# A fused attention, FFN and top-1 expert kernel: the first half of the FFN in five blocks of 256 tokens and two of 512 instead of nine of 256

## The chip, the cores and the metric

The kernel runs on one core of a Trainium2 chip. The metric is the device time of one execution in microseconds (us). Engines are named as in the profile: PE (matrix multiplies; PEld is its weight load), DVE, ACT and POOL (elementwise work), SP (issues most transfers). Each engine works through its own instructions in the order in which the program holds them; waits between engines go by semaphores.

## What is computed

```python
def reference(q, k, v, f, w_in, w_out, expert_emb, tau, w1, w2):
    # attention with a forget gate: 4 batches, 8 heads, 576 tokens, head size 64
    scores = q @ k.T / 8 + (cum_i - cum_j)      # cum = cumsum(log f), causal
    x = softmax(scores) @ v                     # -> 2304 tokens x 512
    # FFN, 512 -> 2048 -> 512
    h = x @ w_in
    g = where(h >= 1, h, where(h <= -1, 0, (h + 1)**2 / 4))
    x = g @ w_out
    # top-1 mixture of 8 experts, 512 -> 1024 -> 512
    e = argmax(cosine(x, expert_emb) / tau); p = softmax(...)[e]
    return p * (relu(x @ w1[e]) @ w2[e])
```

All matrices are float32. The program reads `w_in` and `w_out` as float64 and splits each operand of the FFN and expert products into a high and a low part of the type fp32r, so that every product is three matmuls: high by high, high by low, low by high.

## The kernel before

**Stages.** The FFN is cut into two halves of 1024 hidden units each, because the weights of one half fill their buffers: `half0` (names with p: `hp`, `ghp`, `accp`) and `half1` (names with r). Each half passes over all 2304 tokens; `half0` writes its part of the result to DRAM as `x2p`, `half1` adds its own to it. Then `moe` runs the most frequent expert on all tokens (names with m), and small slots correct the others.

**Blocks.** `half0` has nine blocks of `TB` = 256 tokens (`px0` to `px8`), and `half1` and `moe` have five blocks of up to 512 (`WIDE`, `NW` = 5). A hidden chunk is 128 of the 1024 hidden units, so a block has eight (`NF` = 8). `run1` makes the hidden values: for each chunk 12 matmuls (`first`, L882) into a PSUM bank of 512 columns, which holds two chunks of a 256-token block or one chunk of a 512-token block; one filled bank is a *unit*. `run2` multiplies a chunk by the second weights: 12 matmuls into the accumulator (`ffn_second`, L1011). For 256 tokens the accumulator is one tile `acc`; for 512 tokens it is `acc` and `accB`, and `accB` lies in a pool that exists only after the attention.

**One unit's way** is called the hidden chain in this text: ACT reads the bank into `t` (`tp`, L894), DVE makes `g` in two steps (`gp`, L898 and L899), ACT rounds it to its high part (`ghp`, L903), POOL subtracts for the low part (`glp`, L904). There are two banks (`h_b`), one `t` (`t1_b`), one `g` (`t2_b`) and two pairs of `ghp` and `glp` (`g_b`), so a `ghp` waits until the matmuls of the unit two before it are done.

**Loads and results.** The input of a block is loaded from `xs` in DRAM, rounded by ACT and subtracted by DVE: `load_block` with one transfer and one step each for 256 tokens, `load_wide` with four of each for 512. Buffer 0 exists from the start; buffers 1 and 2 lie in the pool `gp`, which opens when the attention is done (`att_ok`, `late_pools`); a wide load takes buffer 2 or buffers 0 and 1 together. A block's result is taken out of PSUM by `ffn_finish0` (`x_0_n`, L1043 and L1044) and stored by `keep`.

**The second half's weights** are converted while `half0` works on its last blocks. There are 16 pieces (`float64_piece`, names `wbr`, `wbx`, `wb`), and each needs, one behind the other: ACT L825, DVE L826, L828, L830 and L832, ACT L836, POOL L837. All pieces share one buffer `wbx` (`wx_b` = 1), so ACT L825 of a piece waits for POOL L837 of the piece before. In this text piece 5 is the fifth.

**What sets the order.** The order of the instructions on every engine is fixed when the program is built: the class `Order` simulates the engines with estimated durations (`mm`, `act`, `dve`, `pool2`, `dma`) and emits an instruction when its simulated engine takes it. Work carries a priority: attention 0 to 1, hidden chains 2, conversion 4, `first` 6, `ffn_second` 6.5. On the chip the emitted order is kept, whatever the durations then are.

## Time and profile before

| | us |
|---|---|
| median of 3 runs | 866.98 (866.78 to 869.88) |
| the profiled execution's own time | 867.16 |
| its span, first to last instruction | 865.6 |
| PE busy | 844.3 |
| DVE, ACT, POOL busy | 464.6, 362.7, 304.2 |
| last matmul of the attention's weighted sum ends | 312.4 |
| first matmul of `half1` starts | 429.6 |

Busy time is a sum over instructions; a busy PE is one that has a matmul in flight. The chain of waits is followed back from the last instruction and names at each step what released it. PE's clock was granted in full over nearly the whole span (0.997).

### The profile page before, as it was taken

The page shows a single profiled execution, that of the slowest core. Times are in us where ns is not written, and L with a number is a line of the kernel's source. Part 1 is how long each engine was busy: PE and PEld are TensorE (multiplying, and loading weights), DVE is VectorE, ACT ScalarE, POOL GpSimd, SP SyncE. Part 2 cuts the span into 40 slices and gives each one's busy share as a digit, 9 for nine tenths or more (in the row PEclk, how much of TensorE's full clock was granted, in tenths as well). Part 3 has the DMA queues.
Part 4 walks back from the last instruction along what each step waited for, and adds up shares of the span by engine and source line. Part 5 has one row for each costly group of instructions (what it writes and reads, how often), then busy time and mean ns, then how long its engine had stood idle before and what let it go on. Part 6 is the DMA issues. An engine that isn't in the chain of part 4 may idle for free.

```text
span 865.6 us, 15076 instructions
## 1 busy us (share of the span) xinstructions
PE 844.3 (98%) x5384; PEld 693.4 (80%) x5384; DVE 464.6 (54%) x1108; ACT 362.7 (42%) x841; POOL 304.2 (35%) x407
## 2 busy tenths in 40 slices
PE   9999998999999999999899999999999999999997
PEld 7665776887777799999888888888898888887685
DVE  7797977666545537777754344467652531212121
ACT  5677766565556644434533243323343121212110
POOL 3566876555544442444432122222210033000000
PEclk9999999999999999999999999999999999999999
DMA  7997666574324235233611133645432111541220
GB/s 145 174 188 180 164 164 154 123 141 119 95 67 122 73 123 110 79 120 98 207 62 49 61 130 112 211 142 183 148 124 85 49 49 49 211 154 50 98 74 25
DMA packets 154251, 101.96 MB, mean 118 GB/s; under 512 B 102802, under 2 KB 125842, under 8 KB 154176
## 3 DMA queue, kind: packets, MB, share of 16 engines
q1 hardware_dynamic: 151008, 96.22, 40.8%
q0 software_dynamic: 2832, 4.22, 1.8%
q8 instruction: 43, 0.70, 0.4%
q10 hardware_dynamic: 336, 0.56, 0.2%
q14 instruction: 32, 0.26, 0.1%
HBM read 76.86 MB, written 24.49 MB: 117 GB/s over the span
## 4 chain that ended last, share of the span: by engine, by line
PE 82%; DVE 9%; POOL 3%; ACT 2%; issue 2%; DMA 2%; SPq 0%; ACTq 0%; DVEq 0%; POOLq 0%
PE hm L882 12%; PE hr L882 12%; PE hp L882 8%; PE accp L1011 7%; PE accr L1011 6%; PE accBr L1011 6%; PE accm L1023 6%; PE accBm L1023 6%; PE SR L534 4%; PE T L614 4%; PE X L654 4%; PE gt L1197 1%; DVE wbx L830 1%; POOL wb L837 1%; PE U L707 1%
## 5 line engine op out<-in xcount | busy, mean ns | idle before, releaser
L904 POOL TENSOR_TENSOR glr<-gr,ghr 128x512 fp32r<-128x512 f32 x36 | 47.3, 1315 | 147.3 <-PE accBr L1011 90.8
L600 POOL TENSOR_SCALAR P<-P,st 128x512 f32<-128x512 f32 (+3 forms) x128 | 77.0, 615 | 38.4 <-DVE st L596 25.1
L882 PE MATMUL hr<-rx,wb 128*128 128x512 f32 (+1 forms) x384 | 89.5, 367 | 0.0
L882 PE MATMUL hm<-mx,wm 128*128 128x512 f32 (+1 forms) x336 | 87.0, 379 | 0.0
L1011 PE MATMUL accp<-ghp,wa 128*128 128x256 f32 x576 | 83.4, 287 | 2.1 <-DVE x_7b L1044 1.7
L589 ACT ACTIVATE P<-P,st 128x512 f32<-128x512 f32 (+3 forms) x128 | 71.4, 559 | 32.8 <-DVE st L584 31.8
L913 DVE SCALAR_TENSOR_TENSOR glm<-hm,ghm 128x512 fp32r<-128x512 f32 x36 | 24.8, 689 | 103.1 <-PE accBm L1023 68.4
L1011 PEld LDWEIGHTS accp<-ghp,wa 128*128 128x128 f32 x576 | 73.7, 190 | 5.4 <-issue 2.2
L912 ACT ACTIVATE ghm<-hm 128x512 fp32r<-128x512 f32 x36 | 21.6, 599 | 132.5 <-PE accBm L1023 120.7
L882 PEld LDWEIGHTS hr<-rx,wb 128*128 128x128 f32 x384 | 65.6, 188 | 13.0
L882 PEld LDWEIGHTS hm<-mx,wm 128*128 128x128 f32 x336 | 61.0, 188 | 14.9 <-issue 3.4
L904 POOL TENSOR_TENSOR glp<-gp,ghp 128x512 fp32r<-128x512 f32 x36 | 48.8, 1357 | 60.7 <-ACT ghp L903 54.2
L584 DVE CUSTOM_DVE_ANT_0 P<-SR,cm 128x512 f32<-128x512 f32 (+3 forms) x96 | 45.1, 485 | 24.8 <-PE SR L534 22.2
L614 PE MATMUL T<-ident,P 128*128 128x128 f32 x320 | 52.4, 278 | 3.5 <-POOL P L600 2.9
L894 ACT ACTIVATE tr<-hr,quarter 128x512 f32<-128x512 f32 x36 | 24.7, 687 | 61.3 <-DVE gr L899 44.4
L634 ACT COPY pt<-T 128x512 f32<-128x512 f32 (+2 forms) x96 | 35.3, 391 | 36.0 <-PE T L614 35.3
L898 DVE SCALAR_TENSOR_TENSOR gr<-tr 128x512 f32<-128x512 f32 x36 | 25.9, 719 | 42.1 <-POOL glr L904 40.5
L614 PEld LDWEIGHTS T<-ident,P 128*128 128x128 f32 x320 | 36.8, 141 | 14.5 <-POOL P L600 6.3
L534 PE MATMUL SR<-kt,qt 64*128 64x384 f32 (+3 forms) x224 | 44.9, 478 | 2.8 <-DVE st L584 2.5
L1011 PE MATMUL accr<-ghr,wb 128*128 128x512 f32 (+1 forms) x160 | 47.0, 375 | 0.0
L1011 PE MATMUL accp<-glp,wa 128*128 128x256 f32 x288 | 46.3, 283 | 0.4 <-POOL glp L904 0.4
L1011 PE MATMUL accBr<-ghr,wb 128*128 128x512 f32 (+1 forms) x160 | 46.5, 372 | 0.0
(355 smaller groups left out, 1871.8 us busy)
## 6 DMA issues: line engine op xcount, KB each, us to landing
cm<-rows SPq DMA_DIRECT2D x24, 256.0 KB, 4.4
rawq<-in_q_dram SPq DMA_DIRECT2D x64, 72.0 KB, 3.9
rawk<-in_k_dram SPq DMA_DIRECT2D x64, 72.0 KB, 3.3
xs<-xT SPq DMA_DIRECT2D x16, 288.0 KB, 2.1
x2n<-nat SPq DMA_DIRECT2D x18, 256.0 KB, 4.9
war<-in_moe_w_in_dram SPq DMA_DIRECT2D x8, 512.0 KB, 4.7
war<-in_moe_w_out_dram SPq DMA_DIRECT2D x8, 512.0 KB, 4.6
rawv<-in_v_dram SPq DMA_DIRECT2D x32, 128.0 KB, 2.7
```

Source lines behind the costliest of these rows:

```text
L534: nc.tensor.matmul(bank[:, j, :w], qt[p, P * c:P * c + P], kt[p, :w], start=True, stop=i >= NSUM)
L584: yield dve(w + 80, lambda: nc.vector.tensor_tensor_reduce(out=pv_, in0=so, in1=m, scale=-0.125, scalar=3e38, op0=ALU.add, op1=ALU.min, ac ...
L589: yield act(w, lambda: nc.scalar.activation(pw, pw, AF.Exp, bias=st[:, n:n + 1], scale=-1.0, accum_out=st[:, 2 + n:3 + n]), 1, 330)
L600: yield pool1(w, lambda: nc.gpsimd.tensor_scalar(pw, pw, st[:, 6 + n:7 + n], 1.0, ALU.mult, ALU.mult), 0)
L614: nc.tensor.transpose(T[:, P * n:P * n + P], p[:, P * kb:P * kb + P], ident)
L634: yield act(n, lambda: nc.scalar.copy(dh, src), 0)
L654: nc.tensor.matmul(X[D * j:D * j + D, P * kb:], vt[:, kb, j], pt[i, j][0][:, 512 * kb:512 * kb + 512 - P * kb], start=(kb == 0), stop=(kb ...
L882: nc.tensor.matmul(oo, a[:, c, cs], x[c], start=(ip == 0 and c == 0), stop=(ip == 2 and c == KC - 1))
L898: yield dve(n, lambda: nc.vector.scalar_tensor_tensor(g, t, 0.5, t, ALU.min, ALU.mult), 2)
L904: yield pool2(n, lambda: nc.gpsimd.tensor_tensor(gl, g, f32(gh), ALU.subtract), 1)
L1011: nc.tensor.matmul(acc[d][:, :w], b[:, fc, P * d:P * d + P], g, start=(fc == 0 and ip == 0 and (not narrow or d % 2 == 0)), stop=(fc == NF ...
L1023: nc.tensor.matmul(acc[a * (4 // na)], g[:, P * a:P * a + P], b[:, fc], start=(fc == 0 and ip == 0), stop=(fc == NF - 1 and ip == 2))
```

## The change

`half0` keeps 256 tokens for its first five blocks and takes the last 1024 tokens as two blocks of 512. These two are loaded by `load_wide`, wait for the whole attention (`att_ok`), use `acc` and `accB`, and store their result with four transfers of 512 columns (`keep_first`).

```diff
+    NARROW = 5
+    FIRST = [(TB * n, TB) for n in range(NARROW)] + [
+        (t, 2 * TB) for t in range(TB * NARROW, NT, 2 * TB)]
...
         def loads(self):
             for n in self.blocks:
-                if self is half0:
+                if self is half0 and n < NARROW:
...
                             acc = psf.tile([P, 4, TB], F32, tag="acc", name=f"acc{self.name}{n}",
                                            bufs=1)
-                            if self is half0:
+                            if self is half0 and n < NARROW:
...
     def ffn_finish0(n, acc):
+        if n >= NARROW:
+            g = yield (x2_b, ((0, 1),))
+            r = wide_r(f"x2_0_{n}")
+            for d in range(KC):
+                if d % 2:
+                    yield dve(2 * TB, lambda: nc.vector.tensor_scalar(r[d], acc[d], 4.0, None,
+                                                                      ALU.mult), 0)
+                else:
+                    yield act(2 * TB, lambda: nc.scalar.mul(r[d], acc[d], 4.0), 0)
+            go(keep_first(n, r, g))
+            return
...
+    def keep_first(n, r, g):
+        t0, w = FIRST[n]
+
+        def put():
+            for c in range(KC):
+                nc.sync.dma_start(x2pa[c, :, t0:t0 + w], r[c])
+        yield dma(P * KC * w * 4, put, 2, k=4)
+        for m in range(t0 // TB, (t0 + w) // TB):
+            done(x2p_ok[m])
+        give(x2_b, g)
...
-    half0 = Layer("p", [TB] * NB, lambda: W0, xs, xs_ok, ffn_hidden, ffn_second, ffn_finish0, 6)
+    first_ok = xs_ok[:NARROW] + [att_ok] * (len(FIRST) - NARROW)
+    half0 = Layer("p", [w for _, w in FIRST], lambda: W0, [xsa[:, :, t:t + w] for t, w in FIRST],
+                  first_ok, ffn_hidden, ffn_second, ffn_finish0, 6)
```

In this text the two wide blocks are called block 5 and block 6 of the changed kernel, and their units are u0 to u7 of each. The order on PE is the same in both programs up to the middle of block 4's second products. Lines of the changed kernel are 3 higher up to `run2`, and 14 or 25 higher behind it.

On PE, before, at the point where the two orders part: `px5` is the input of the sixth block, `accp` with `ghp_2` and `ghp_4` are second products of block 4.

```order
L1011 MATMUL accp_4302<-glp_2_4247,wa_98 128x256 x4
L882 MATMUL hp_0_4385<-px5h,wa_96 128x256 x8
L882 MATMUL hp_0_4385<-px5h,wa_97 128x256 x4
L1011 MATMUL accp_4302<-ghp_2_4246,wa_98 128x256 x4
L1011 MATMUL accp_4302<-ghp_2_4246,wa_99 128x256 x4
L1011 MATMUL accp_4302<-glp_2_4247,wa_98 128x256 x4
L882 MATMUL hp_0_4385<-px5h,wa_96 128x256 x8
L882 MATMUL hp_0_4385<-px5h,wa_97 128x256 x4
```

On PE, after, five half units of 12 matmuls behind the same point: block 4 is finished first, and then come the wide units. `pse` is a small transpose for the experts, whose input comes from DVE.

```order
L1014 MATMUL accp_4305<-glp_6_4421,wa_98 128x256 x4
L885 MATMUL hp_0_4471<-px_4285,wa_96 128x512 x8
L885 MATMUL hp_0_4471<-px_4285,wa_97 128x512 x4
L885 MATMUL hp_1_4497<-px_4285,wa_96 128x512 x8
L885 MATMUL hp_1_4497<-px_4285,wa_97 128x512 x4
L885 MATMUL hp_2_4518<-px_4285,wa_96 128x512 x8
L885 MATMUL hp_2_4518<-px_4285,wa_97 128x512 x4
L1198 MATMUL pse<-ident,em 128x8 x4
L885 MATMUL hp_3_4551<-px_4285,wa_96 128x512 x8
L885 MATMUL hp_3_4551<-px_4285,wa_97 128x512 x4
L1014 MATMUL accp_4568<-ghp_0_4538,wa_98 128x512 x2
```

Block 4's second products and block 5's first products no longer alternate, and `pse` stands behind the third wide unit.

On DVE, before, at piece 2 of the conversion (`wbx`), whose first step stands ahead of `ie`, the copy that waits for `pse`:

```order
L898 SCALAR_TENSOR_TENSOR gp_2_4535<-tp_2_4516 128x512
L826 TENSOR_SCALAR wbx<-wbx 128x512
L899 SCALAR_TENSOR_TENSOR gp_2_4535<-tp_2_4516,gp_2_4535 128x512
L1175 COPY ie<-pse 128x4x8
L828 TENSOR_SCALAR wbx<-wbx 128x512
L830 SCALAR_TENSOR_TENSOR wbx<-wbr,wbx 128x512
L832 SCALAR_TENSOR_TENSOR wbx<-wbr,wbx 128x512
```

On DVE, after, at the same piece 2; `px_4355` is block 6's input:

```order
L871 TENSOR_TENSOR px_4355<-px_4355 128x512
L1200 COPY ie<-pse 128x4x8
L829 TENSOR_SCALAR wbx<-wbx 128x512
L901 SCALAR_TENSOR_TENSOR gp_1_4567<-tp_1_4540 128x512
L871 TENSOR_TENSOR px_4355<-px_4355 128x512
L902 SCALAR_TENSOR_TENSOR gp_1_4567<-tp_1_4540,gp_1_4567 128x512
L831 TENSOR_SCALAR wbx<-wbx 128x512
L833 SCALAR_TENSOR_TENSOR wbx<-wbr,wbx 128x512
L835 SCALAR_TENSOR_TENSOR wbx<-wbr,wbx 128x512
```

Piece 2 moved behind the copy of `pse`, and one step of block 6's input stands inside it.

On ACT, after, from the first step of piece 2 (L828) to the last ACT step of piece 3 (the second L839):

```order
L828 ACTIVATE wbx<-wbr 128x512
L870 CAST px_4355<-px_4355 128x512
L906 CAST ghp_1_4586<-gp_1_4567 128x512
L897 ACTIVATE tp_2_4588<-hp_2_4518,quarter 128x512
L839 CAST wb_4265<-wbx 128x512
L906 CAST ghp_2_4614<-gp_2_4598 128x512
L897 ACTIVATE tp_3_4616<-hp_3_4551,quarter 128x512
L828 ACTIVATE wbx<-wbr 128x512
L906 CAST ghp_3_4653<-gp_3_4636 128x512
L897 ACTIVATE tp_4_4655<-hp_4_4594,quarter 128x512
L839 CAST wb_4263<-wbx 128x4x128
```

The same stretch of ACT before:

```order
L825 ACTIVATE wbx<-wbr 128x512
L894 ACTIVATE tp_4_4572<-hp_4_4515,quarter 128x512
L1043 ACTIVATE x_0_4a<-accp_4302 128x512
L903 CAST ghp_2_4589<-gp_2_4535 128x512
L836 CAST wb_4265<-wbx 128x512
L825 ACTIVATE wbx<-wbr 128x512
L894 ACTIVATE tp_6_4646<-hp_6_4571,quarter 128x512
L903 CAST ghp_4_4676<-gp_4_4626 128x512
L836 CAST wb_4263<-wbx 128x4x128
```

Two hidden chains now stand between the last steps of piece 2 and piece 3, where there was one. Behind piece 3 both programs alternate one piece and one unit, up to piece 13 (before, two units stand together once, between pieces 10 and 11).

On DVE, after, at the end of `half0`: behind piece 13 come the chains of block 6's u6 and u7, among the steps of the second half's first input `rx` and of piece 14.

```order
L835 SCALAR_TENSOR_TENSOR wbx<-wbr,wbx 128x512
L901 SCALAR_TENSOR_TENSOR gp_6_5141<-tp_6_5109 128x512
L902 SCALAR_TENSOR_TENSOR gp_6_5141<-tp_6_5109,gp_6_5141 128x512
L871 TENSOR_TENSOR rx_5101<-rx_5101 128x512
L901 SCALAR_TENSOR_TENSOR gp_7_5167<-tp_7_5159 128x512
L829 TENSOR_SCALAR wbx<-wbx 128x512
L871 TENSOR_TENSOR rx_5101<-rx_5101 128x512
L902 SCALAR_TENSOR_TENSOR gp_7_5167<-tp_7_5159,gp_7_5167 128x512
L831 TENSOR_SCALAR wbx<-wbx 128x512
```

The same place before:

```order
L832 SCALAR_TENSOR_TENSOR wbx<-wbr,wbx 128x512
L898 SCALAR_TENSOR_TENSOR gp_4_5462<-tp_4_5403 128x512
L899 SCALAR_TENSOR_TENSOR gp_4_5462<-tp_4_5403,gp_4_5462 128x512
L826 TENSOR_SCALAR wbx<-wbx 128x512
L828 TENSOR_SCALAR wbx<-wbx 128x512
L898 SCALAR_TENSOR_TENSOR gp_6_5523<-tp_6_5485 128x512
L830 SCALAR_TENSOR_TENSOR wbx<-wbr,wbx 128x512
L868 TENSOR_TENSOR rx_5442<-rx_5442 128x512
L899 SCALAR_TENSOR_TENSOR gp_6_5523<-tp_6_5485,gp_6_5523 128x512
```

One more step of `rx` stands ahead of the last unit's second step. Behind `half0`, PE runs four first units of `half1` before its first `accr` in the kernel before, and three in the changed one; behind `half1`'s third block both orders are the same.

## Rows read from the trace of the kernel before

**Rows 1.** The page, part 1: busy us, share of the span and instructions by engine.

```profile
PE 844.3 (98%) x5384; PEld 693.4 (80%) x5384; DVE 464.6 (54%) x1108; ACT 362.7 (42%) x841; POOL 304.2 (35%) x407
```

**Rows 2.** Stretches: length, busy us by engine, clock, DMA share, GB/s.

```profile
312.40:331.20 18.80, 18.80 (x157) 18.80 (x158) 10.19 (x13) 8.36 (x13) 7.80 (x15) 1.00 0.72 159
331.20:429.60 98.40, 94.07 (x774) 92.48 (x773) 71.00 (x99) 44.60 (x75) 43.38 (x29) 1.00 0.42 129
429.60:520.00 90.40, 90.40 (x406) 73.51 (x405) 42.91 (x84) 31.03 (x63) 21.89 (x17) 1.00 0.23 76
```

**Rows 3.** PE in order of time: start us, us, engine, line, what, [idle before].

```profile
323.94 1.58 PE L882 MATMUL hp<-px5h,wa 128*128 128x256 f32 x12
...
345.89 1.12 PE L1011 MATMUL accp<-ghp,wa 128*128 128x256 f32 x8
...
347.33 0.64 PE L882 MATMUL hp<-px6h,wa 128*128 128x256 f32 x4
...
429.58 10.65 PE L882 MATMUL hr<-rx,wb 128*128 128x512 f32 x45
...
443.57 2.96 PE L882 MATMUL hr<-rx,wb 128*128 128x512 f32 x12
...
446.37 0.63 PE L1011 MATMUL accr<-ghr,wb 128*128 128x512 f32 x2
```

**Rows 4.** PE in order of time: two rows ahead of which PE waited.

```profile
378.93 1.68 PE L882 MATMUL hp<-px7h,wa 128*128 128x256 f32 x12 [0.73 <-ACT tp L894]
...
427.57 0.74 PE L1011 MATMUL accp<-glp,wa 128*128 128x256 f32 x4 [0.43 <-POOL glp L904]
```

**Rows 5.** The chain of waits, one round of the conversion: start us, us, what.

```profile
379.25 0.67 ACT wbx L825
...
380.87 1.68 DVE wbx L830
382.57 0.70 DVE wbx L832
383.30 0.63 ACT wb L836
...
384.00 1.73 POOL wb L837
...
385.75 0.67 ACT wbx L825
```

**Rows 6.** POOL in order of time.

```profile
342.87 1.30 POOL L837 TENSOR_TENSOR wb<-wbx,wb 128x512 fp32r<-128x512 f32 x1
...
380.55 1.44 POOL L904 TENSOR_TENSOR glp<-gp,ghp 128x512 fp32r<-128x512 f32 x1 [1.34 <-ACT ghp L903]
...
390.50 1.72 POOL L837 TENSOR_TENSOR wb<-wbx,wb 128x512 fp32r<-128x512 f32 x1 [2.01 <-ACT wb L836]
...
397.34 1.75 POOL L837 TENSOR_TENSOR wb<-wbx,wb 128x512 fp32r<-128x512 f32 x1 [2.00 <-ACT wb L836]
...
418.67 1.75 POOL L837 TENSOR_TENSOR wb<-wbx,wb 128x512 fp32r<-128x512 f32 x1 [1.28 <-ACT wb L836]
...
436.10 1.30 POOL L837 TENSOR_TENSOR wb<-wbx,wb 128x512 fp32r<-128x512 f32 x1 [6.89 <-ACT wb L836]
```

**Rows 7.** DVE in order of time.

```profile
346.27 0.69 DVE L830 SCALAR_TENSOR_TENSOR wbx<-wbr,wbx 128x512 int32<-128x512 int32 x1
...
424.47 0.69 DVE L899 SCALAR_TENSOR_TENSOR gp<-tp,gp 128x512 f32<-128x512 f32 x1
```

**Rows 8.** ACT in order of time.

```profile
330.15 1.05 ACT L851 CAST px6h<-px6l 128x1024 fp32r<-128x1024 f32 x1 [0.40 <-DMA px6l<-xs]
...
425.25 0.62 ACT L903 CAST ghp<-gp 128x512 fp32r<-128x512 f32 x1 [3.07 <-DVE gp L899]
...
436.01 0.62 ACT L903 CAST ghr<-gr 128x512 fp32r<-128x512 f32 x1
```

**Rows 9.** SP in order of time: the issue of a transfer.

```profile
320.77 0.37 SPq L848 DMA_DIRECT2D px6l<-xs  x1
```

## The prediction, made before the result was known

> **What bounds the kernel now.** I read the busy times first: PE has a matmul in flight for 844.3 of 865.6 us [rows 1], so a change pays only where it shortens PE's work or PE's waits. Then the stretches [rows 2]: of the 98.40 us from 331.20 to 429.60, in which the blocks run that the change touches, PE is busy 94.07, while behind them it has no gap at all (90.40 of 90.40). So the change must act inside this stretch, and whatever it moves there goes through to the end one to one.
>
> The 4.3 us of PE waits in the stretch say little by themselves; what they wait for says more. One wait is for `tp`, a step of the hidden chain, and the last one, just ahead of the end, for `glp`, its last step [rows 4]. Followed back, the chain of waits does not run over PE here but over the conversion of the second half's weights, round after round [rows 5]: ACT L825 at 379.25, DVE L826 and L828, L830 for 1.68, L832 for 0.70, ACT L836 for 0.63, POOL L837 for 1.73, and the next L825 at 385.75. A round takes 6.50 us, and the order on ACT, DVE and POOL puts one unit's hidden chain into each round. PE needs 1.44 us for a half unit of 256 columns (345.89 to 347.33) [rows 3], so 5.76 for the four that make and use one unit. A round is longer. PE lives on the units that it is ahead, and when these are used up it waits. **The stretch is bound by the conversion's round at its end, with PE close behind.** That is the point on which this change turns.
>
> **What the change takes from PE.** The parting point is 323.94 [rows 3]; up to there both orders are the same. Afterwards PE finishes block 4 with five half units, 323.94 + 5 x 1.44 = 331.14, and then has 16 wide units with 32 groups of 12 matmuls. Such a group takes 2.80 us (443.57 to 446.37) [rows 3], against 2.88 for two half units: 32 x 0.08 = 2.6 us saved. With some 0.4 for `pse` (four short matmuls, an estimate at a third of a half unit's twelve) PE alone could start `half1` at 331.14 + 0.4 + 32 x 2.80 = 421.1 instead of 429.58 [rows 3]. That is 8.5 us less: 2.6 of work, 4.3 of waits, the rest small gaps around waits. It is the most the change can give, and it comes only if the other engines keep up.
>
> **What it does to the chain.** The work on ACT, DVE and POOL is nearly the same: 16 units of 512 columns before and after, 16 pieces, the same elements loaded and stored, in smaller steps. Loading `px` for block 5 is hidden: it has from about 315 to 331 and PE is busy with block 4. What counts is when the pieces run. I follow them by the changed order, with the steps of the rows: L826 and L828 0.46 each (1.62 from 379.25 to 380.87, less 0.70 for L825), other DVE steps 0.6 to 0.7, and 1.7 for one that meets a POOL step (L830: 0.69 alone [rows 7], 1.68 while `glp` runs from 380.55 [rows 5, 6]); from an ACT step to the next engine 0.7.
>
> Piece 2: its first DVE step now stands behind `ie`, which waits for `pse` behind the third wide unit: 331.14 + 3 x 2.80 + 0.4 = 339.9. With the copy, two steps of `gp`, one of `px`, its own four and one meeting, L832 ends at 345.3, and L837 starts at 346.0; before it was 342.87 [rows 6]. **3.1 us late.**
>
> Piece 3: ACT has two `ghp` in front of its L836. The second waits for a pair of `ghp` and `glp`, thus for the second products of u1: 339.9 + 4 x 2.80 = 351.1. Behind it come `tp` and L836, and on POOL that unit's `glp` goes first: L837 at 353.7.
>
> Piece 4: L825 at 355.0, and DVE, held up by that L837, takes `gp` of u4 first, to 356.2. Then 0.46 + 0.46 + 0.7 + 1.7, and 0.7 on ACT: L837 at 360.2.
>
> Pieces 5 to 13: one piece and one unit each, in the order of the steady rounds of before. Eight rounds at 6.50 and one at 7.1, in which two results of block 5 leave the accumulators (with one result a round took 6.84, 390.50 to 397.34 [rows 6]): 360.2 + 52.0 + 7.1 = 419.3. **Before, piece 13 stood at 418.67 [rows 6].** The lateness of 3 us is won back almost wholly, since the steps that load block 6 no longer fall into the rounds. But a wide unit costs PE 5.60 and a round 6.50. When piece 4 runs, PE still has some 7 us in hand; that lead goes at 0.9 a unit, and block 5's accumulators, emptied by DVE only behind piece 9's steps, take 2 us of it too. From the middle of block 6 PE waits for the chain again.
>
> The end: behind piece 13 come u6 and u7. L837 ends at 420.9, `glp` of u6 at 422.2; on DVE a step of `rx` ends at 422.9, then `gp`, L826, another `rx` and the second `gp`: 425.4, against 425.16 before (424.47 + 0.69) [rows 7]. `ghp` at 425.5, against 425.25 [rows 8]; 0.7 later PE starts the last group of 12: 426.2 + 2.80 = 429.0. **`half1` starts at 429.0 instead of 429.58: a gain of 0.6.**
>
> The start of `half1`: before, four first units ran ahead of the first `accr`, and `ghr` was there at 436.01 [rows 8], 4 us early. Now three run ahead, so PE wants it at 429.0 + 3 x 2.80 = 437.4. In front of it stand on ACT both results of block 6 and L836 of piece 15. On DVE seven steps lead to the end of piece 14 (425.4 + 7 x 0.6 + one meeting of 1.0 = 430.6), then L836, L837 and L825 take 0.7 + 1.3 + 0.7 (the 1.30 of POOL at 436.10 [rows 6]), and eight DVE steps of 0.6 lead to the second `gr`: 438.2. With 0.1 and 0.7 PE starts at 439.0: a new wait of 1.6. Behind that, each later unit has its chain in time, as before.
>
> **The sum.** 867.16 (the profiled execution's own time) - 0.6 + 1.6 = 868.2. That execution stands 0.18 over the median of 866.98, so 868.0 as a median of runs. Bounds: if piece 4 runs at PE's pace and not behind DVE (L837 at 358.3) 1.9 are gained, and without the wait at the first `accr` another 1.6: 864.5. If all nine rounds take 6.84, 9 x 6.84 - 59.1 = 2.5 are lost, and a doubled wait adds 1.6: 872.1. I take the middle since the rows with the same order of steps gave 6.50.
>
> **Rivals.**
> (B) *PE sets the pace.* A round is long because `glp` starts on POOL just ahead of L830 on DVE and doubles it [rows 5, 6]. Where `ghp` waits for PE, `glp` comes later; if that keeps it off L830 and L832, the round is 6.50 - 0.99 = 5.51, less than PE's 5.60, PE never waits, and the whole 8.5 us come: 867.0 - 8.5 = 858.5, or 860.5 with 2 us at block 5's accumulators; I say 859.5. It decides where a freed round stays under 5.60. Against it: as soon as PE has a lead, `ghp` does not wait for it, and the meeting is back; steady rounds before all had it. [...]
>
> (C) *Slower: block 6's input lands late.* Before, a transfer of 512 KB issued at 320.77 [rows 9] was still waited for at 330.15 [rows 8], at 159 GB/s with the DMA engines 0.72 busy [rows 2]. Now 512 KB more stand in front of it and it is itself 1 MB: two times 0.5 MB at 159 GB/s, 3.3 us each, so the last part lands at 336.7. ACT reaches the first of its casts at 332.6, and two of them stand ahead of `tp` of u0. If the four parts land in order, the first two come at about 331.5 and 333 and nothing waits; if they share the engines and land together, ACT stands 4 us, PE waits for its bank, and pieces 2 to 13 move by 4: 868.0 + 4 = 872. It decides from a landing of the second part later than 334. For it: the wait of 0.40 at 330.15 shows the transfers to be the last to come there. Against it: the four are issued one behind the other, 0.37 apart at least [rows 9], and none is needed before the one issued ahead of it.
>
> That the change doesn't do what it says, on PE, I exclude: the order shows 512 columns in each of the 384 matmuls.
>
> **How the numbers follow.** Forecast (A, the round stays the bound) 0.74; B 0.12; C 0.14. About 0.5% (4.3 us) is what a measurement of this kernel can tell from no change: faster means under 862.7, slower over 871.3. A lies within it but for its top, 0.05. So faster 0.12, same 0.69, slower 0.19. The range of 8 in 10 is A's bounds with a little on the lower side, for a chain freed in some rounds only: 863.5 to 872.3.
>
> **What would show it.** Right: PE busy less by 2 to 3 us in sum, and a first matmul of `half1` at 427 to 431; the chain of waits from about 360 to 420 over L825 to L837 with rounds of 6.5; PE gaps that wait for `tp` or `ghp` in block 6, one of 1 to 2 us for block 5's accumulators, one ahead of the first `accr`. Piece 2 at 346, piece 4 at 360, piece 13 at 419. Wrong: rounds of 5.6 and no gaps in block 6 (B); ACT waiting for a transfer of `px6` near 333, with `tp` of u0 at 338 instead of 334.5 (C). I would be wrong too if the first wide unit started later than 331.5.

## The result, and the profile after

The changed kernel is slower: 873.35 us (median of 8 runs, 869.88 to 875.07) against 867.17 for the kernel before in the same series, a ratio of 1.0061 with a 95% interval of 1.004 to 1.0082. The forecast was 868.0, with a range up to 872.3. The profiled execution of the changed kernel took 871.14, its span 869.5. Lines up to `run2` are 3 higher than before: L828 to L840 are a piece of the conversion, L897 `tp`, L901 and L902 `gp`, L906 `ghp`, L907 `glp`, L870 and L871 the steps of an input; L1014 are the second products, L1048 a DVE step that empties an accumulator.

The busy times (the page, part 1) answer to [rows 1]; below them, one view on, the three stretches of [rows 2] (length, busy us by engine with counts, clock, DMA share, GB/s).

```profile
PE 844.2 (97%) x5000; PEld 674.6 (78%) x5000; DVE 466.9 (54%) x1112; ACT 362.4 (42%) x845; POOL 309.8 (36%) x407
```

```profile
312.40:331.20 18.80, 18.76 (x153) 18.42 (x152) 10.29 (x14) 7.02 (x13) 7.69 (x14) 1.00 0.70 214
331.20:429.60 98.40, 91.19 (x382) 71.67 (x380) 72.64 (x103) 44.23 (x76) 46.67 (x29) 0.97 0.36 107
429.60:520.00 90.40, 89.07 (x393) 72.43 (x393) 41.46 (x80) 30.32 (x61) 23.99 (x18) 0.98 0.26 87
```

384 matmuls are gone, and yet PE is as long busy as before (844.2 against 844.3). In the middle stretch it has 7.2 us without a matmul where it had 4.3, and two numbers that stood at 1.00 have fallen: the granted clock is 0.97 there and 0.98 behind it. Cut smaller, the clock of these stretches has fallen in two places only:

```profile
427.00:434.00 7.00, 4.90 (x12) 3.37 (x11) 4.49 (x8) 3.01 (x6) 5.57 (x2) 0.51 0.24 75
392.00:397.00 5.00, 5.00 (x15) 3.89 (x16) 3.23 (x5) 1.75 (x3) 2.10 (x2) 0.66 0.88 284
```

In the first the clock was 0.50 from 427.5 to 433.5, in the second it was 0.50 from 393 to 396, and from 434 and from 397 it was 1.00 again. Half clock means this 0.50 from here on. Both places stand behind waits of PE, as its rows show in order of time (start us, us, engine, line, what, [idle before]):

```profile
308.94 2.37 PE L657 MATMUL X<-pt,rawv 128*64 128x512 f32 x16
...
392.00 0.73 PE L1014 MATMUL accBp<-ghp,wa 128*128 128x512 f32 x2 [1.82 <-DVE x_1b L1048]
...
393.93 1.05 PE L1014 MATMUL accp<-glp,wa 128*128 128x512 f32 x2
...
425.96 0.74 PE L1014 MATMUL accp<-ghp,wa 128*128 128x512 f32 x2 [2.07 <-ACT ghp L906]
...
430.93 1.22 PE L1014 MATMUL accp<-glp,wa 128*128 128x512 f32 x2 [2.10 <-POOL glp L907]
...
432.81 9.07 PE L885 MATMUL hr<-rx,wb 128*128 128x512 f32 x36
441.71 0.63 PE L1014 MATMUL accr<-ghr,wb 128*128 128x512 f32 x2
```

At 393.93 a pair of matmuls takes 1.05 instead of the 0.62 to 0.63 of undisturbed pairs. The last unit of `half0` waits twice, 2.07 for its `ghp` and 2.10 for its `glp`. `half1` starts at 432.81; before it was 429.58 [rows 3].

POOL in order of time holds the forecast's pieces, and the place where it broke:

```profile
345.14 1.75 POOL L840 TENSOR_TENSOR wb<-wbx,wb 128x512 fp32r<-128x512 f32 x1 [1.28 <-ACT wb L839]
...
352.41 1.29 POOL L840 TENSOR_TENSOR wb<-wbx,wb 128x512 fp32r<-128x512 f32 x1
...
358.97 1.75 POOL L840 TENSOR_TENSOR wb<-wbx,wb 128x512 fp32r<-128x512 f32 x1 [1.28 <-ACT wb L839]
...
419.51 1.74 POOL L840 TENSOR_TENSOR wb<-wbx,wb 128x512 fp32r<-128x512 f32 x1 [1.29 <-ACT wb L839]
421.21 1.29 POOL L907 TENSOR_TENSOR glp<-gp,ghp 128x512 fp32r<-128x512 f32 x1
426.04 4.84 POOL L907 TENSOR_TENSOR glp<-gp,ghp 128x512 fp32r<-128x512 f32 x1 [3.53 <-issue]
```

Pieces 2, 3, 4 and 13 came at 345.14, 352.41, 358.97 and 419.51. The last row is the last unit's `glp`: 4.84 us for a step that took 1.29 just ahead of it. DVE in order of time shows what ran beside it:

```profile
425.46 0.68 DVE L871 TENSOR_TENSOR rx<-rx 128x512 fp32r<-128x512 f32 x1
426.06 0.68 DVE L871 TENSOR_TENSOR rx1l<-rx1l,rx1h 128x512 fp32r<-128x512 f32 x1
426.66 0.68 DVE L833 SCALAR_TENSOR_TENSOR wbx<-wbr,wbx 128x512 int32<-128x512 int32 x1
427.26 0.68 DVE L871 TENSOR_TENSOR rx<-rx 128x512 fp32r<-128x512 f32 x1
427.87 0.68 DVE L871 TENSOR_TENSOR rx1l<-rx1l,rx1h 128x512 fp32r<-128x512 f32 x1
428.47 0.68 DVE L835 SCALAR_TENSOR_TENSOR wbx<-wbr,wbx 128x512 int32<-128x512 int32 x1
429.07 0.68 DVE L871 TENSOR_TENSOR rx<-rx 128x512 fp32r<-128x512 f32 x1
430.36 1.07 DVE L871 TENSOR_TENSOR rx<-rx 128x512 fp32r<-128x512 f32 x1 [0.60 <-ACT rx L870]
```

Seven DVE steps with two inputs stand one behind the other, each at its normal 0.68. They are not held up; POOL is. Only when DVE pauses for 0.60, waiting for ACT, does `glp` get through: it ends at 430.88, and now the next DVE step, at 430.36, is the one that takes longer (1.07).

In the kernel before, the last unit's `glp` took 1.51. This is its row, with the two rows of PE between which the next paragraph measures:

```profile
426.00 1.51 POOL L904 TENSOR_TENSOR glp<-gp,ghp 128x512 fp32r<-128x512 f32 x1 [3.99 <-ACT ghp L903]
...
310.01 2.37 PE L654 MATMUL X<-pt,rawv 128*64 128x512 f32 x16
...
440.77 0.63 PE L1011 MATMUL accr<-ghr,wb 128*128 128x512 f32 x2
```

**A measure for comparing kernels.** From the first `accr` to the issue of the last store all kernels of this study need the same 421.9 us (863.60 - 441.71 in the changed kernel; before, 859.92 - 440.77 = 419.15, with one group of `hr` more ahead of `accr`, 2.80 [rows 3]). So I compare the way from the end of the attention's last weighted sum to the first `accr`: 441.71 - (308.94 + 2.37) = 130.4 here, and 440.77 - 312.38 - 2.80 = 125.6 before. **The change lengthens that way by 4.8 us; behind it PE needs the same time.** The attention itself ended 1.07 us earlier in this execution (311.31 against 312.38), so the spans differ by less than the ways.

PE's rows on the way give the parts: its waits add up to 8.4 us where they were 4.2, the matmuls need 2.6 less (the prediction's sum), the 5 us at 0.66 lost some 1.7, and the half clock behind the two last waits some 1.4 (four matmuls took 1.88 us from 430.93 to 432.81 and need 0.93 at full speed, by the 2.80 for 12 of [rows 3]; 36 `hr` took 8.90 and need 8.40). 4.2 - 2.6 + 1.7 + 1.4 = 4.7.

### The profile page after: what moved, and what is told of

The parts are those of the page before. It is cut to its first block, busy times and chain, and to the rows that moved or that the text cites. A ratio compares the mean times of both kernels' runs of the same rounds, so it can differ in the third digit from the quotient of the medians.

```text
span 869.5 us, 14316 instructions
## 1 busy us (share of the span) xinstructions
PE 844.2 (97%) x5000; PEld 674.6 (78%) x5000; DVE 466.9 (54%) x1112; ACT 362.4 (42%) x845; POOL 309.8 (36%) x407
## 4 chain that ended last, share of the span: by engine, by line
PE 84%; DVE 6%; POOL 3%; issue 2%; ACT 2%; DMA 1%; SPq 0%; POOLq 0%; DVEq 0%; ACTq 0%
PE hr L885 12%; PE hm L885 12%; PE accp L1014 7%; PE hp L885 7%; PE accr L1014 6%; PE accBr L1014 6%; PE accm L1026 6%; PE accBm L1026 6%; PE SR L537 5%; PE X L657 4%; PE T L617 4%; PE warm L734 2%; POOL wb L840 2%; PE SR L532 1%; PE gt L1222 1%
## 5 line engine op out<-in xcount | busy, mean ns | idle before, releaser
L907 POOL TENSOR_TENSOR glr<-gr,ghr 128x512 fp32r<-128x512 f32 x36 | 47.1, 1308 | 151.6 <-PE accBr L1014 74.3
L907 POOL TENSOR_TENSOR glp<-gp,ghp 128x512 fp32r<-128x512 f32 x36 | 53.4, 1483 | 53.7 <-ACT ghp L906 44.2
L1014 PE MATMUL accp<-ghp,wa 128*128 128x256 f32 (+1 forms) x384 | 67.7, 309 | 2.2 <-ACT ghp L906 2.1
L1014 PEld LDWEIGHTS accp<-ghp,wa 128*128 128x128 f32 x384 | 52.6, 190 | 8.3 <-ACT ghp L906 3.0
L901 DVE SCALAR_TENSOR_TENSOR gr<-tr 128x512 f32<-128x512 f32 x36 | 25.9, 718 | 48.0 <-POOL glr L907 27.6
L897 ACT ACTIVATE tr<-hr,quarter 128x512 f32<-128x512 f32 x36 | 24.7, 687 | 58.9 <-PE hr L885 29.1
L1014 PE MATMUL accr<-ghr,wb 128*128 128x512 f32 (+1 forms) x160 | 47.0, 375 | 0.0
L1014 PE MATMUL accBr<-ghr,wb 128*128 128x512 f32 (+1 forms) x160 | 46.5, 372 | 0.0
L1026 PE MATMUL accm<-wm,ghm 128*128 128x512 f32 x144 | 46.2, 394 | 0.0
```

Source lines behind the costliest of these rows:

```text
L901: yield dve(n, lambda: nc.vector.scalar_tensor_tensor(g, t, 0.5, t, ALU.min, ALU.mult), 2)
L907: yield pool2(n, lambda: nc.gpsimd.tensor_tensor(gl, g, f32(gh), ALU.subtract), 1)
L1014: nc.tensor.matmul(acc[d][:, :w], b[:, fc, P * d:P * d + P], g, start=(fc == 0 and ip == 0 and (not narrow or d % 2 == 0)), stop=(fc == NF ...
L1026: nc.tensor.matmul(acc[a * (4 // na)], g[:, P * a:P * a + P], b[:, fc], start=(fc == 0 and ip == 0), stop=(fc == NF - 1 and ip == 2))
```

## The experiments

### The same again, and the two visible culprits

The first four kernels ran beside the kernel before at 866.69.

**The changed kernel once more** (no edit).

> The changed kernel once more, as the reference of this batch. Theory (waits of PE plus half clock behind them): 871 to 875 us, stretches at half clock again behind the wait for block 5's accumulators and behind the waits of the last unit, at slightly other places; the time varies with how long they last. Rival (something that the first profile does not show, such as a longer attention): the start of the second half at 433 or earlier and the excess elsewhere.

872.24 us, ratio 1.0077 (1.0049 to 1.0105), the way 130.6. Its last `glp` took 4.84 again, from 426.12, and DVE's pause ahead of its end was 0.60 again. The loss is the kernel's, not one execution's. The first spell of half clock did not come back, other than expected: from 390 to 400 the clock was 1.00, behind the same wait of 1.8 for block 5's accumulators, and what PE won there it waited behind it (10.5 us in sum instead of 8.4). The way is the same, so that spell cost nothing that counts. PE was busy 842.2 us here, 2.1 less than before. The second spell did come back: from 430 to 440 the clock was 0.83, and the 36 `hr` took 9.94.

**The steps of `rx` behind the last `glp`.** DVE subtracts for `half1`'s input only when the last unit's chain is done:

```diff
             yield act(w, lambda: nc.scalar.copy(hi[c][:, :w], f32(lo[c])[:, :w]), 1)
+            if name.startswith("rx"):
+                yield half0.g_ok[6, (7,)]
             yield dve(w, lambda: nc.vector.tensor_tensor(
```

> The changed kernel, but DVE takes the subtractions of the second half's first two inputs only after the last unit's glp has started its way. Theory (the glp of the last unit, 4.84 us instead of 1.3, was held off by ten DVE steps in a row): glp takes 1.3 to 2.3, the wait of 2.10 for it goes, the second half starts at 429 to 430 instead of 432.8; 2.5 to 4 us less than the changed kernel. Rival (the conversion's rounds alone set the end, and PE's other waits take the clock anyway): at most 1 us less.

872.64 us, ratio 1.0078 (1.0055 to 1.0102): no gain. The last `glp` took 1.38 us, and `half1` starts as early as hoped for, but only with two matmuls. PE in order of time:

```profile
426.67 0.83 PE L887 MATMUL hr<-rx,wb 128*128 128x512 f32 x2
...
429.38 0.49 PE L887 MATMUL hr<-rx,wb 128*128 128x512 f32 x1 [1.88 <-ACT rx L870]
...
430.90 9.47 PE L887 MATMUL hr<-rx,wb 128*128 128x512 f32 x33 [1.02 <-ACT rx L870]
```

It then waits for the very steps that were put off, and the clock was lower behind these waits (0.83 from 430 to 440): the last 33 matmuls need 9.30 us up to `accr` instead of 7.70. The way is 129.4: of the 3.5 us that `glp` lost, 1.0 is won. The forecast of 2.5 to 4 failed. The same DVE work has to be done ahead of `half1`, before `glp` or behind it.

**Filling PE's waits,** with useless matmuls of 128 columns into a spare bank ahead of three of the waiting groups, to keep the clock up. The program holds 14, 17 and 17 of them; the trace counts 28, 34 and 34, and a row of 17 lasted 3.96 us, 0.23 each where 0.11 was meant:

```diff
...
         for ip, (b, g) in enumerate(((bh, gh), (bl, gh), (bh, gl))):
+            for _ in range({0: late["fill"][0], 2: late["fill"][1]}.get(ip, 0)):
+                nc.tensor.matmul(late["X"][:, :P], ident, ident, start=True, stop=True)
             for d in range(KC):
...
```

> The changed kernel with small matmuls of no use put into three waits of PE: 14 ahead of block 6's first second products, 17 ahead of the last unit's, 17 in the middle of it, some 0.11 us each. Their result is not used. Theory (part of the loss is the clock, which fell to half behind these waits): the clock is granted in full from 385 to 440, the three waits become busy and no longer, 2 to 3 us less than the changed kernel, and less spread between executions. Rival (the waits alone cost, the clock is a mere sign): the time is that of the changed kernel or 1 us more.

874.37 us, ratio 1.0095 (1.0073 to 1.0117): 2.1 more than the changed kernel beside it, more than either reading had expected. The granted clock was 1.00 from 390 to 400 and from 410 to 440 (0.83 between, behind a wait of 1.83), and yet `half1` starts at 434.45, with its 36 matmuls at full speed:

```profile
434.45 8.56 PE L885 MATMUL hr<-rx,wb 128*128 128x512 f32 x36
```

The way is 131.3. The last row of fillers ran until 433.44, 2.9 us after `glp` was done (425.64 + 4.86 = 430.50), so this run doesn't price the clock, and it doesn't show that the clock is free. What it shows is that `glp` takes as long (4.86) at a full clock.

**A second buffer for the converted weights** in the changed kernel, so that a piece no longer waits for the piece before:

```diff
-        x = fp.tile([P, DM], I32, tag="wx", name=name + "x", bufs=1)
+        x = (late["gp"].tile([P, DM], I32, tag="nat", name=name + "x", bufs=2) if gx[0] else
+             fp.tile([P, DM], I32, tag="wx", name=name + "x", bufs=1))
...
         give(late["gl_b"], g)
         done(setup_ok)
+        give(wx_b, [1])
```

> The changed kernel with two buffers wbx instead of one, so that a piece's first step need not wait for the last step of the piece before. Theory (the round of 6.5 us bounds the stretch): pieces overlap, PE does not wait in block 6, the second half starts at 421 to 425, and 8 to 10 us come off the changed kernel: 863 to 866. Rival (DVE and POOL themselves are full, one buffer is not the reason): the rounds stay at 6 us or more and at most 2 us come off.

869.6 us, ratio 1.0039 (1.0027 to 1.0052), the way 127.4. It is 2.6 us better than the changed kernel beside it, far from the 8 to 10 that the removal of the bound named in the prediction should give, and PE waits almost as much as in the changed kernel (7.9 us against 8.4), once for 3.41 us. DVE, POOL, ACT and PE in order of time, ahead of that wait:

```profile
384.57 1.50 POOL L908 TENSOR_TENSOR glp<-gp,ghp 128x512 fp32r<-128x512 f32 x1 [2.93 <-ACT ghp L907]
...
385.06 1.31 DVE L830 TENSOR_SCALAR wbx<-wbx 128x512 f32<-128x512 f32 x1
...
386.03 1.46 POOL L841 TENSOR_TENSOR wb<-wbx,wb 128x512 fp32r<-128x512 f32 x1
...
386.39 1.38 DVE L832 TENSOR_SCALAR wbx<-wbx 128x512 int32<-128x512 int32 x1
...
389.70 0.69 ACT L898 ACTIVATE tp<-hp,quarter 128x512 f32<-128x512 f32 x1 [4.12 <-DVE gp L903]
...
390.44 0.94 PE L886 MATMUL hp<-px6h,wa 128*128 128x512 f32 x2 [3.41 <-ACT tp L898]
```

Two POOL steps stand side by side here and hold off two DVE steps, 1.31 and 1.38 instead of 0.43. `gp` stands behind these on DVE, `tp` waits for `gp`, and PE for `tp`. The round of one buffer is gone, and what remains is the meeting of DVE with POOL.

### What the stretch is bound by

From here on four readings stand against each other in the expectations. **S**: DVE's and POOL's steps hold each other off (1.31 and 1.38 instead of 0.43 above, 4.84 instead of 1.29 in the changed kernel), and their common time fills the stretch; PE's blocks hardly matter. **E**: the loss sits only where `half1` takes over from a wide block. **B**: the chain over the one buffer alone is the bound (the prediction's own reading, its forecast A; not its rival B). **L**: what counts is how long the chain of a piece or unit is by itself.

For S speaks a sum. I take each step of DVE and POOL at the shortest time that its line shows. Before, from 330.0 to 429.58, these are 26 one-input steps of `wbx` at 0.41, 26 with two at 0.69, 13 `wb` at 1.30, 30 `gp` at 0.67, 16 `glp` at 1.28, and some 10 us of others: 96.1 us in a stretch of 99.6. In the changed kernel, from 329.3 to 432.81, they are 101.4 in 103.5. By this sum both are nearly full, and the order of the changed kernel put 5.3 us more of this work ahead of `half1`: four more steps of `rx` (2.7), most of piece 14 (two steps of 0.69 and a `wb`, 2.7) and two more `gp` (1.4), with 1.6 less in loads and results. `half1` starts 4.3 later (432.81 - 311.31 = 121.5 against 429.58 - 312.38 = 117.2). The rows themselves, overlaps counted once, have at least one of the two engines at work in 89.4 of the 99.6 us before and in 93.3 of the 103.5 in the changed kernel, and in 10.2 us of either stretch neither works. So the stretch isn't full in the strict sense; but of the 4.3 us, 3.9 are time in which DVE or POOL worked. That this work is the cause is argued so far, not shown. The next four kernels ran beside the kernel before at 868.33.

**The second buffer in the kernel before** (the same edit as above).

> The kernel before with a second buffer for the converted weights (`wbx`). Theory S (DVE's two-input steps and POOL's steps exclude each other, so that one piece and one unit take at least the sum of both, 2 x 0.44 + 4 x 0.69 + 2 x 1.29 = 6.2 us, whatever PE's blocks are): rounds fall from 6.5 to 6.9 towards 6.2, but not below, PE's waits in front of half1 shrink by 1 to 3 us, so 864 to 866 against 866.7. The same kernel with wide blocks and two buffers took 869.6, so narrow would stay ahead of wide by 4 or more. Theory E (the loss sits only in the take-over of half1 from a wide block): the second buffer is worth as much here as in the wide kernel, 2.6 us, so 864. Theory B (one buffer's chain alone is the bound): rounds fall to PE's 5.76 and all 4.3 us of waits go, 862.5.

872.45 us, ratio 1.0056 (1.0037 to 1.0076): slower than without it, by 4 us, which no reading had expected. The way is 130.5. Two of PE's waits:

```profile
384.26 1.86 PE L883 MATMUL hp<-px7h,wa 128*128 128x256 f32 x12 [1.86 <-ACT tp L895]
...
423.55 1.22 PE L1012 MATMUL accp<-ghp,wa 128*128 128x256 f32 x8 [2.11 <-DVE x_7b L1045]
```

The pieces do come sooner: the thirteenth's `wb` starts at 408.37, where it was 418.67 [rows 6], and the fifteenth's at 418.92. But each piece drawn forward takes DVE and POOL from the units' chains, and the units are what PE waits for. B falls with this; one buffer had been a useful brake. S as I had put it, with rounds and a small gain, was wrong in sign here; that DVE and POOL are the scarce thing fits (some 103 us of steps ahead of `half1`, in 104.1), but is not shown by this run.

**The last step of pieces and chains on DVE,** in both kernels. POOL's `wb` (1.29) of the second half's weights and its `glp` from block 5 on become DVE steps of 0.69. DVE has more to do, but no POOL step is left beside it:

```diff
-        yield pool2(DM, lambda: nc.gpsimd.tensor_tensor(lo, xv, f32(hi), ALU.subtract), prio)
+        if name == "wb":
+            yield dve(DM, lambda: nc.vector.tensor_tensor(lo, xv, f32(hi), ALU.subtract), prio)
+        else:
+            yield pool2(DM, lambda: nc.gpsimd.tensor_tensor(lo, xv, f32(hi), ALU.subtract), prio)
...
-        yield pool2(n, lambda: nc.gpsimd.tensor_tensor(gl, g, f32(gh), ALU.subtract), 1)
+        if nm[0] == "p" and int(nm[1]) >= 5:
+            yield dve(n, lambda: nc.vector.tensor_tensor(gl, g, f32(gh), ALU.subtract), 1)
+        else:
+            yield pool2(n, lambda: nc.gpsimd.tensor_tensor(gl, g, f32(gh), ALU.subtract), 1)
```

In the kernel before:

> The kernel before with the last step of each piece of the second half's weights and of each unit's chain from block 5 on moved from POOL (1.29 us) to DVE (0.69 us): no POOL step runs beside DVE's in the stretch, and a round needs 2 x 0.44 + 6 x 0.69 = 5.0 us of DVE. Theory S: rounds near 5.5, below PE's 5.76 for a unit of narrow blocks, so PE's waits of 4.3 us in the stretch go almost wholly: 862.5 to 864. Theory E: little changes, 866 to 867, since DVE has more to do and nothing is taken from the take-over of half1.

In the changed kernel:

> The changed kernel with the same move: the last step of each piece and of each unit's chain from block 5 on goes from POOL to DVE. Theory S: with rounds near 5.5, below PE's 5.60 for a wide unit, PE sets the pace, the 2.6 us of matmul time that the change saves show up, and the half clock and the waits of 8.4 us go: 859 to 861, that is 2 to 4 us under the same edit in the kernel before. Theory E: the take-over of half1 stays late (last chain behind the steps of rx, accumulators of a wide block, first accr one unit earlier), so 868 to 872 and 3 to 6 us over the same edit in the kernel before.

**863.74 us (ratio 0.9958, 0.9942 to 0.9973) with narrow blocks, and 860.18 (0.9908, 0.988 to 0.9936) with wide ones.** Both beat the kernel before by little, but clear of the interval, and the order of the two is turned round: wide is now 3.6 us faster. Both times lie in S's ranges (862.5 to 864 and 859 to 861). The ways are 121.1 and 116.8. PE in order of time, narrow:

```profile
308.67 2.38 PE L654 MATMUL X<-pt,rawv 128*64 128x512 f32 x16
...
412.20 1.21 PE L1017 MATMUL accp<-ghp,wa 128*128 128x256 f32 x8 [1.41 <-DVE x_7b L1050]
...
432.16 0.63 PE L1017 MATMUL accr<-ghr,wb 128*128 128x512 f32 x2
```

and wide:

```profile
312.77 2.38 PE L657 MATMUL X<-pt,rawv 128*64 128x512 f32 x16
...
423.13 5.76 PE L888 MATMUL hr<-rx,wb 128*128 128x512 f32 x24
429.09 3.06 PE L888 MATMUL hr<-rx,wb 128*128 128x512 f32 x12 [0.19 <-ACT tr L900]
431.98 0.63 PE L1020 MATMUL accr<-ghr,wb 128*128 128x512 f32 x2
```

The wide kernel's lead of 4.3 us on the way is, to 0.3, the 2.6 that the change saves on matmuls plus the 1.41 that only the narrow kernel still waits, for its single accumulator. In the wide kernel PE has a matmul in flight for 98.11 of the 98.40 us, and a round takes 5.50 where no other work falls into it (DVE in order of time, one `wb` to the next), under PE's 5.60:

```profile
331.20:429.60 98.40, 98.11 (x438) 79.81 (x438) 84.43 (x147) 49.70 (x85) 0.92 (x1) 1.00 0.43 122
```

```profile
377.26 0.68 DVE L841 TENSOR_TENSOR wb<-wbx,wb 128x512 fp32r<-128x512 f32 x1
...
382.76 0.68 DVE L841 TENSOR_TENSOR wb<-wbx,wb 128x512 fp32r<-128x512 f32 x1
```

DVE itself does 147 steps in these 98.40 us, where it did 103 beside POOL. E falls: the take-over of `half1` from a wide block costs nothing here but the 0.19 ahead of its third group.

**One wide block only** (`NARROW = 7`, seven blocks of 256 and the last of 512).

> The changed kernel with seven blocks of 256 tokens and one of 512, that is the last block alone is wide. Theory S: half of the matmul time is saved and none of it counts; the loss follows how the chains and the pieces fall, and is about half of the change's, 868 to 871. Theory E (the loss is that of half1's start behind a wide block, paid once): as the change itself, 871 to 874. A third reading (the loss is block 5's start, with its lost lead and the late second piece): 866 to 868.

871.69 us, ratio 1.0048 (1.0026 to 1.0071), the way 127.6. The time lies within E's range (871 to 874) and 0.7 above S's (868 to 871), so taken alone it speaks for E rather than for S; E has fallen by the run before. PE waits 3.04 us in `half1`'s first unit, for ACT's step of `rx` (`hr` at 427.54), as when `rx` was put off.

### Shared time, or a shorter chain?

Moving a step from POOL to DVE also shortens the chains, by 0.6 each time (reading L). The last four kernels ran beside the kernel before at 867.45. In two of them the chains stay short and POOL gets its work back as a useless step of the old size beside each moved one. Nobody waits for it (not printed: the same call beside `wb`, and the tile):

```diff
+    def pool_load(prio):
+        if "load" in late:
+            d = late["dum"]
+            yield pool2(DM, lambda: nc.gpsimd.tensor_tensor(d, d, d, ALU.subtract), prio)
...
+            go(pool_load(1))
             yield dve(n, lambda: nc.vector.tensor_tensor(gl, g, f32(gh), ALU.subtract), 1)
...
```

> The changed kernel with the last step of pieces and chains on DVE, as measured at 860.2, plus a useless POOL step of the old size (128x512, two inputs, into a tile that nobody waits for) beside each of them. The chains are as short as without it; only POOL's work is back. Theory S (DVE's and POOL's steps exclude each other and their sum is the stretch): DVE is held off again, for about 30 steps of 1.29 us now on top of DVE's longer work (83 + 39 us of steps for a stretch of 93), so PE's waits return and the time goes up by 10 to 25 us, to 870 to 885. Theory L (the gain came from the shorter chain of a piece and a unit, 0.69 us on DVE instead of 1.29 on POOL): 859 to 862.

> The same useless POOL steps in the kernel before with the last steps on DVE, as measured at 863.7. Theory S: bound by the sum of DVE and POOL again, 870 to 885, and the wide blocks are no faster than the narrow ones any more (wide less narrow between -1.5 and +5, where without POOL's steps it was -3.6). Theory L: 862 to 865, and wide still 3 to 4 faster.

**876.08 us with wide blocks and 876.02 with narrow ones** (ratios 1.0086, 1.0056 to 1.0115, and 1.0102, 1.0076 to 1.0128). The gain is gone and 8.6 us more, and wide is no longer faster, as S had it (870 to 885 for both). In the traces PE, DVE and ACT take their own steps from the end of the attention to the first `accr` in the same order as without the load, so a change of order is not behind it. The useless steps were not spread as meant: as they wait for nothing, POOL ran them one behind the other, up to some 380. That makes the wide kernel's stretches (columns as above) the clearest of the study:

```profile
340.00:360.00 20.00, 15.94 (x64) 12.30 (x63) 19.76 (x20) 5.75 (x10) 18.92 (x14) 0.91 0.21 69
360.00:380.00 20.00, 12.57 (x50) 9.67 (x49) 19.05 (x17) 4.98 (x8) 17.25 (x13) 0.92 0.17 52
380.00:400.00 20.00, 20.00 (x81) 16.21 (x80) 18.65 (x32) 9.80 (x16) 0.00 (x0) 0.91 0.29 88
```

Beside 14 and 13 POOL steps DVE does 20 and 17 steps in 20 us, and PE runs dry; with POOL still, DVE does 32 and PE is full. The DVE rows show how:

```profile
349.37 1.52 DVE L911 SCALAR_TENSOR_TENSOR gp<-tp,gp 128x512 f32<-128x512 f32 x1
350.82 1.52 DVE L847 TENSOR_TENSOR wb<-wbx,wb 128x512 fp32r<-128x512 f32 x1
```

Both steps, 0.69 alone, take 1.52: one per POOL step. L falls as the only cause, since the chains consist of the same steps as in the fast kernels; that the shorter chains had a part in the gain is not excluded. Two more bounds of this pair: the load was denser than in the real kernels, so the 12 to 16 us between the pairs are not its price there; and a pair of steps took about 1.45 (349.37 to 350.82), not 0.69 + 1.29, so the sum of both engines' steps is a measure of how full the stretch is and no strict limit. That they exclude each other, as the expectations word S, was an assumption and is not shown.

**The last three pieces behind the last chain.** This takes away part of the work that the changed order had put ahead of `half1`:

```diff
                 yield times[n]
+                if W.name == "wb" and n >= 13:
+                    yield half0.g_ok[6, (7,)]
                 g = yield (wr_b, 1)
```

In the kernel before the same line names its last unit, `[8, (6, 7)]`.

> The changed kernel with the last three pieces of the second half's weights started only when the last unit of half0 has its chain behind it. Theory S: piece 14's steps (6 on DVE and POOL that stand ahead of half1's start, about 4.5 us of the shared time) move behind it, so the last unit's chain ends earlier by up to that: half1 starts 2 to 4 us earlier, 868 to 871 against 872 to 873 for the changed kernel. Rival: the steps of rx alone hold the last chain, so 872 to 873.

> The same in the kernel before. Theory S: there only four DVE steps of piece 14 stand ahead of the last unit's chain and its POOL step waits for nothing, so less is to be had: 0 to 2.5 us, 864.5 to 867.5 against about 867. Rival: as much as in the wide kernel, 863 to 865.

868.58 us with wide blocks (ratio 1.0004, 0.9988 to 1.0019; the way 126.1) and 865.91 with narrow ones (0.9988, 0.9976 to 1.0; the way 124.5). Both times lie where S had them. The changed kernel wins 4.3 us on the way, the kernel before 1.1. POOL and PE of the wide one in order of time:

```profile
425.70 1.55 POOL L909 TENSOR_TENSOR glp<-gp,ghp 128x512 fp32r<-128x512 f32 x1 [3.16 <-ACT ghp L908]
```

```profile
426.19 1.19 PE L887 MATMUL hr<-rx,wb 128*128 128x512 f32 x4 [1.57 <-ACT rx L872]
...
437.48 0.63 PE L1016 MATMUL accr<-ghr,wb 128*128 128x512 f32 x2
```

`glp` is back at 1.55, and `half1` now waits for the steps of `rx` alone. Some 3 us (4.3 less 1.1) are thus what the edit brings in the changed kernel alone. Not all of it need be the pieces' own time: the new order also puts `half1`'s first unit ahead of the last second products (423.76 against 429.12), and the last 24 `hr` need 5.60 us up to `accr` (431.88 to 437.48), as at full speed, where the changed kernel lost some 1.4 to the half clock. 1.6 are left between the two kernels.

All kernels side by side:

| kernel | median us | ratio to before | the way, us | against before |
|---|---|---|---|---|
| before | 867.17 | 1 | 125.6 | |
| changed | 873.35 | 1.0061 | 130.4 | +4.8 |
| changed, once more | 872.24 | 1.0077 | 130.6 | +5.0 |
| changed, `rx` later | 872.64 | 1.0078 | 129.4 | +3.8 |
| changed, waits filled | 874.37 | 1.0095 | 131.3 | +5.7 |
| changed, two buffers | 869.60 | 1.0039 | 127.4 | +1.8 |
| changed, late pieces | 868.58 | 1.0004 | 126.1 | +0.5 |
| one wide block | 871.69 | 1.0048 | 127.6 | +2.0 |
| before, two buffers | 872.45 | 1.0056 | 130.5 | +4.9 |
| before, late pieces | 865.91 | 0.9988 | 124.5 | -1.1 |
| before, last steps on DVE | 863.74 | 0.9958 | 121.1 | -4.5 |
| changed, last steps on DVE | 860.18 | 0.9908 | 116.8 | -8.8 |
| the same with POOL loaded, before | 876.02 | 1.0102 | 133.8 | +8.2 |
| the same with POOL loaded, changed | 876.08 | 1.0086 | 133.2 | +7.6 |

## Why the prediction was wrong

**The side was right, the size too small.** It called the 8.5 us of PE's possible gain out of reach and forecast +1.0; +6.2 was measured.

**What PE needs: right.** The first wide matmul came at 330.37 (forecast 331.14). The 2.6 us of matmul time exist: they show as soon as POOL is out of DVE's way. There `half1` started 423.13 - 315.15 = 108.0 us behind the attention; the prediction's figure for PE alone is 421.1 - 312.38 = 108.7. The sign "PE busy less by 2 to 3 us" did not come in the profiled execution (844.2), as matmuls at half clock took longer; in the second one it did (842.2).

**When the pieces run: right at the start, by luck at the end.** Piece 2 came at 345.14 (346.0), piece 3 at 352.41 (353.7), piece 4 at 358.97 (360.2); counted from the attention's end, which came 1.07 earlier here, these three are met to 0.2. Of the nine rounds behind piece 4 six took 6.5, but all nine took 60.54 where the sum had 59.1: one took 7.87, one 6.85, one 6.69. That piece 13 stood at 419.51 (419.3) is two errors that cancel, the early attention and the longer rounds. The wait at block 5's accumulators was 1.82 (2).

**The end: the step that failed.** "0.7 later PE starts the last group of 12: 426.2 + 2.80 = 429.0." The group started at 425.96. But its last four matmuls need `glp`, and the step silently took `glp` to be there in time: it stood at 426.04 and was done at 430.88, because DVE ran seven two-input steps in a row. I had the order of these steps before me (I counted the `rx` steps ahead of the second `gp`), but looked only at what stands ahead of `gp` on DVE and not at what runs beside `glp` behind it. I had priced a meeting of the two engines as POOL delaying DVE (1.68 against 0.69 [rows 5, 7]) and never the other way round. `half1` started at 432.81, 3.8 late: at full speed PE would have wanted `glp` at 425.96 + 8 x 0.2333 = 427.83 and could go on at 430.93, 3.1 later, and its last four matmuls ran at half clock (1.88 instead of 0.93).

**The clock: left out.** I named no half clock. From 427 to 434 it was 0.51, behind the waits of 2.07 and 2.10; on the way this cost some 1.4 us, 0.9 in these four matmuls and 0.5 in the 36 `hr`. In the second execution the `hr` alone lost 1.5 (9.94 against 8.40). No run has a long wait for `glp` without the half clock or the fillers, so the clock is priced by rows only.

**The wait at the first `accr`: did not come.** With `half1` starting later, its chain was in time. So 439.0 became 441.71, and 868.2 plus these 2.7 is 870.9 for the profiled execution, which took 871.14. That this fits so well is partly luck too, since the attention ended 1.07 early: from its end to `accr` the prediction had 439.0 - 312.38 = 126.6, and 130.4 was measured, 3.8 more.

**The bound of the stretch: named too narrowly.** The round over one buffer was the visible chain, but two buffers slowed the narrow kernel down and gave the wide one only 2.6. What was scarce is DVE and POOL together. My own rows held a sign of it: DVE 71.00 and POOL 43.38 us busy in 98.40 [rows 2], that is 114 in sum for two engines that hold each other off (a step that is held off counts as busy, as L830's 1.68 does [rows 5], so the sum can be more than the stretch).

**The rivals.** The prediction's B had a right cause (`glp` on POOL beside L830 on DVE) and the wrong hope, that a shifted start would free it. Taking POOL out gave 860.18, close to B's 859.5, but by another edit and not by the change. C did not happen: block 6's input was there in time, and PE ran without a wait from 330.37 to 386.

**What stays open.** The profiled ways differ by 4.8 us, the profiled times by 4.0 (871.14 against 867.16), the medians by 6.2. The two profiled executions of the changed kernel (871.14 and 871.48) lie low among its twelve (869.88 to 875.51). The longest of them have the lowest mean clock (0.989 to 0.990 for all over 874), so spells at half clock that the two traces don't hold are a likely part; I have no trace of such an execution. Traces of other kernels have a longer attention together with a lower clock, outside the way: with wide blocks and the last steps on DVE the page shows the clock between 0.8 and 0.9 from 129 to 151, where it was 0.9 or more in the changed kernel, and the attention ended at 315.15 instead of 311.31. One execution took 873.02 at a mean clock of 0.996, so the clock is not all of it; the last store, with its two durations 2 us apart (below), is another candidate that wasn't tested. How the 4.8 us divide between DVE's and POOL's time, the starved `glp` and the half clock is open as well, since no run changes one of them alone.

## What to carry to other kernels

Where two engines hold each other off, add up both engines' steps over the stretch before believing a chain of waits: here DVE and POOL, busy 71 and 43 of 98 us, left little room together. A cheaper matmul did not help, a second buffer gave 2.6 us in one kernel and took 4 in the other, while moving POOL's steps to the "busier" DVE took 4.5 us off the way with narrow blocks and 13.6 with wide ones. A scheduler that fills a gap with work that isn't due yet can push the one chain that is due behind it; with wide blocks, holding three pieces back was worth 4 us. And look at what runs beside a step on the other engine, not only at what stands ahead of it in its own queue.

## What the runs showed of the hardware

- **A row of DVE steps starved a POOL step.** `glp` (two inputs, 128x512) took 4.84 us instead of 1.29 beside seven two-input DVE steps of 0.68 without a gap, and got through in the first pause, of 0.60 us; so it was in both executions of the changed kernel, and 4.86 with PE's waits filled. In the other direction, with the useless POOL steps one behind the other (24 in 34.58 us), each let one DVE step through (1.52 instead of 0.69). A single meeting made one DVE step take 1.68 instead of 0.69 [rows 5, 7]. What decides which side is held off, and for how long, the traces do not show.
- **One-input DVE steps were held off too.** L830 and L832 in the kernel with two buffers, TENSOR_SCALAR on 128x512 of 32 bits, took 1.31 and 1.38 beside POOL instead of 0.43.
- **The last store had two durations.** From its issue to the end of the span the traces show 5.6 to 6.0 us in eight of them and 7.2 to 8.1 in the other six (5.90 in the changed kernel, 8.01 with `rx` later, 7.67 with wide blocks and the last steps on DVE), with the same transfer of 256 KB, which landed 2.0 us after its issue in the changed kernel and 3.8 in the last of these. This is why spans were not compared with each other here; its cause was not looked for.
